# Remainder indices in a mixed-radix Fourier filter: one matrix per transform stage, in a kernel with a mixture of experts behind it

## The chip, the cores and the metric

The kernel runs on one core of a Trainium2 chip. The metric is the device time of one execution in microseconds (us). The core's engines, as the profile names them, are PE (TensorE: matrix products; PEld is its weight load), DVE (VectorE), ACT (ScalarE), POOL (GpSimd) and SP (SyncE, which here only issues DMAs, in the order of its queue). All data is 32-bit floating point.

## What is computed

The input `x` has 8 batches of 2496 tokens with 256 channels. First every channel of a batch is filtered along the tokens by a Fourier transform; then each token goes through the one expert, of eight, that its logits choose, and the result is weighted with the softmax value of that expert.

```python
X = np.fft.rfft(x, axis=1)                       # 8 x 2496 x 256
Y = X * (filt_r + 1j * filt_i)[None, :, :]
y = np.fft.irfft(Y, n=2496, axis=1).reshape(19968, 256)
logits = y @ w_gate                              # 256 x 8
e = np.argmax(logits, axis=1)
gate = softmax(logits)[token, e]                 # sum + 1e-9
out[token] = gate * (np.maximum(y[token] @ w1[e], 0) @ w2[e])   # 256 -> 1024 -> 256
```

## The kernel before

**Transform.** 2496 = 39 x 64 (`N1`, `N2`). Because `x` is real, 20 (`NF`) of the 39 frequencies of the short axis are enough. A batch passes four stages, each a set of matrix products with a constant matrix as the stationary operand:

- Stage A (`stage_a`, L344): the transform over 39, for three of the 64 offsets at a time, 22 columns (`NG`) of 117 rows in six chunks (`CH`); matrix `tas`, one for all columns; 512 moving elements per product. The result goes to DRAM (`zd`).
- Stage B (`stage_b`, L359): the transform over 64, for one frequency f of the 20 at a time. The twiddle factors are folded into the matrix, so `tbs` holds 20 matrices and each product moves 256 elements; two frequencies share a PSUM bank. DVE then multiplies by the filter `ht`: `ys` with the real part (L366), `yw` with the imaginary part in two halves of the partitions (L367, L368), and the sum of both at L370, on POOL in batch 0 and on DVE later.
- Stage C (`stage_c`, L382 and L384): back over 64, with `tcs`, which holds one matrix for f = 0 and one for the others, so the first pair is two products of 256 and the other nine pairs are one of 512. The result goes to DRAM (`ud`).
- Stage D (`stage_d`, L405): back over 39 with twiddles, 22 matrices in `tds`, products of 256 elements; the result lies in the buffers `yo` (tag "y", six of them).

Batch 0 doesn't go through DRAM: `first_a` (L424), `turn_z` (L441), `first_c` (L449) and `turn_u` (L464) turn the data with transposes on PE. Behind D come the logits (L491), the routing (`route`, small DVE instructions), and for each of a batch's columns a scatter of rows by POOL (L607) into `rowsd`, sorted by expert.

**Experts.** Tiles of 512, 256 or 128 sorted rows are read back (`xg`), transposed (L737), multiplied with `w1` (`hidden`, L744, with the ReLU on ACT at L748) and `w2` (`result`, L758), and the rows are scattered to `out` (L764).

**What sets the order.** PE, DVE, ACT and SP run an order that a planner writes while the program is built. It walks through `STEPS` (filter work: each has a place, a load that it needs, and a cost) and `experts()`; `now`, `credit` and `share()` decide which goes next. `more_loads` issues loads of `x`, `z` and `u` as long as fewer than `NIN` = 7 of them are held (buffers tag "in"); `halt` keeps steps that load `u` or use `y` back when all six `yo` buffers are held (`held_y[0] == 6`). POOL's order is set by the framework's scheduler. `load_filters(c)` runs between the steps of `first_a`: for four frequencies it loads part of `tbs` (L255), the real part of the filter (L256) and the imaginary part (L260, L262). `load_rest` loads `tds` (L267) and small constants.

Of the kernel before, what the change touches and what calls it, by code (L numbers as in the profile page):

```python
# [10 lines left out]
F32 = mybir.dt.float32  # L11
# [3 lines left out]
ALU = mybir.AluOpType  # L15
# [4 lines left out]
P = 128  # L20
S = 2496
D = 256
E = 8
F = 1024

N1 = 39
N2 = 64
NF = (N1 + 1) // 2
NS = 2 * NF

NB = 3
NG = 22
TP = NB * N1
TK = NB * NS
# [1 line left out]
FT = F // P  # L36


def dft_tables():

    w = 2.0 * np.pi
    q = np.arange(N1)
    t = np.arange(N2)
    g = np.arange(N2)  # L50
    half = N2 // 2
    sg = np.where(g < half, 1.0, -1.0)

    ta = np.zeros((NB, N1, NB, NS))
    for f in range(NF):
        ang = w * ((q * f) % N1) / N1
        for j in range(NB):
            ta[j, :, j, f] = np.cos(ang)
            if f:
                ta[j, :, j, NF + f] = -np.sin(ang)  # L60

    tb = np.zeros((2, N2, NF, 2, N2))
    for f in range(NF):
        ang = w * ((t[:, None] * (f + N1 * g)[None, :]) % S) / S
        c, sn = np.cos(ang), np.sin(ang)
        if f:
            tb[0, :, f, 0] = c
            tb[1, :, f, 0] = sn
            tb[0, :, f, 1] = -sn * sg
            tb[1, :, f, 1] = c * sg  # L70
        else:
            tb[0, :, f, 0, :half] = c[:, :half]
            tb[0, :, f, 1, 1:half] = -sn[:, 1:half]
            tb[0, :, f, 0, half] = (-1.0) ** t

    tc = np.zeros((2, N2, 2, 2, N2))
    ang = w * ((g[:, None] * t[None, :]) % N2) / N2
    c, sn = np.cos(ang), np.sin(ang)
    tc[0, :, 1, 0] = c
    tc[0, :, 1, 1] = sn  # L80
    tc[1, :, 1, 0] = -sn * sg[:, None]
    tc[1, :, 1, 1] = c * sg[:, None]
    tc[0, :half, 0, 0] = 2.0 * c[:half]
    tc[1, :half, 0, 0] = -2.0 * sn[:half]
    tc[1, 0, 0, 0] = 0.0
    tc[0, 0, 0, 0] = 1.0
    tc[0, half, 0, 0] = (-1.0) ** t

    td = np.zeros((NB, NS, NG, NB, N1))
    ids = np.zeros((NB, N1, NG))  # L90
    valid = np.zeros((NB, N1, NG))
    for j in range(NB):
        for i in range(len(range(j, N2, NB))):
            n = N2 * q + NB * i + j
            ids[j, :, i] = n
            valid[j, :, i] = 1.0
            td[j, 0, i, j] = 1.0 / S
            for f in range(1, NF):
                ang = w * ((n * f) % S) / S
                td[j, f, i, j] = 2.0 / S * np.cos(ang)  # L100
                td[j, NF + f, i, j] = -2.0 / S * np.sin(ang)

    return {
        "ta": ta.reshape(TP, TK),
        "tb": tb.reshape(P, NF, P),
        "tc": tc.reshape(P, 2, P),
        "td": td.reshape(TK, NG, TP),
        "ids": ids.reshape(TP, NG),
        "valid": valid.reshape(TP, NG),
    }  # L110


def lay_x(x):

    out = np.zeros((x.shape[0], P, NG, D), x.dtype)
    v = x.reshape(-1, N1, N2, D)
    for j in range(NB):
        n = len(range(j, N2, NB))
        out[:, j * N1:(j + 1) * N1, :n] = v[:, :, j::NB]
    return out  # L120


def lay_filter(fr, fi):

    g = np.arange(N2)[:, None]
    f = np.arange(NF)[None, :]
    k = f + N1 * g
    k = np.where(k <= S // 2, k, S - k)
    fr, fi = fr[k], fi[k]
    h = NF // 2  # L130
    return np.concatenate([np.concatenate([fr, fr]), np.concatenate([fi[:, :h], fi[:, h:]])], axis=1)
# [3 lines left out]
def kernel(  # L135
# [8 lines left out]
    tb: bass.AP,  # L144
    tcm: bass.AP,
    td: bass.AP,
    ids: bass.AP,
    valid: bass.AP,
    out: bass.AP,
):  # L150
    nc = tc.nc
    mm = nc.tensor.matmul
# [24 lines left out]
    DR = D + 16  # L177
# [15 lines left out]
    psr = fft.enter_context(tc.tile_pool(name="psr", bufs=1, space=PSUM))  # L193

    tas = cst.tile([TP, TK], F32, name="tas")
    tbs = cst.tile([P, NF, P], F32, name="tbs")
    tcs = cst.tile([P, 2, P], F32, name="tcs")
    tds = cst.tile([TK, NG, TP], F32, name="tds")

    ht = cst.tile([P, NF + NF // 2, D], F32, name="ht")  # L200

# [46 lines left out]
    HP = P // 2  # L248
# [3 lines left out]

    def load_filters(c):
        f0, n = FH[c]
        nc.sync.dma_start(out=tbs[:, f0:f0 + n], in_=tb[:, f0:f0 + n])  # L255
        nc.sync.dma_start(out=ht[:HP, f0:f0 + n], in_=filt[:HP, f0:f0 + n, :])  # L256
        half, f1 = divmod(f0, NF // 2)
        rows = slice(half * HP, (half + 1) * HP)
        nh = min(n, NF // 2 - f1)
        nc.sync.dma_start(out=ht[rows, NF + f1:NF + f1 + nh], in_=filt[rows, NF + f1:NF + f1 + nh, :])  # L260
        if nh < n:
            nc.sync.dma_start(out=ht[HP:, NF:NF + n - nh], in_=filt[HP:, NF:NF + n - nh, :])  # L262
        if c == 0:
            nc.sync.dma_start(out=tcs, in_=tcm)

# [33 lines left out]
            yield NS, slice(m, n), rows[(NG - 1) * TK:, :].rearrange("(i p) d -> p i d", p=NS)  # L299

    ins, outs, lgs, yts = {}, {}, {}, {}
    NIN = 7

    moves, stored = [[], []], set()

# [45 lines left out]
    def stage_b(b, f):  # L351
        c, j = divmod(f, 4)
        if b == 0:
            zi, j = outs.pop(("zi", f)), 0
        else:
            zi = ins["z", b, c] if j == 0 else ins.pop(("z", b, c))
        p = bank()
        for i in range(2):
            mm(p[:, i * D:(i + 1) * D], lhsT=tbs[:, f + i, :], rhs=zi[:, j + i, :], start=True, stop=True)  # L359

        z2 = p.rearrange("p (i d) -> p i d", i=2)
        ys = outs["y", b, f] = sb.tile([P, 2, D], F32, tag="ys", name="ys", bufs=3)
        yw = sb.tile([P, 2, D], F32, tag="yw", name="yw")
        half, f1 = divmod(f, NF // 2)
        fi = ht[half * HP:(half + 1) * HP, NF + f1:NF + f1 + 2, :]
        nc.vector.tensor_mul(ys, z2, ht[:, f:f + 2, :])  # L366
        nc.vector.scalar_tensor_tensor(out=yw[:HP], in0=z2[HP:], scalar=-1.0, in1=fi, op0=ALU.mult, op1=ALU.mult)  # L367
        nc.vector.tensor_mul(yw[HP:], z2[:HP], fi)  # L368

        (nc.gpsimd if b == 0 else nc.vector).tensor_tensor(ys, ys, yw, op=ALU.add)  # L370
        free["v"] = max(free["v"], now[0]) + (2.1 if b == 0 else 2.8)

    def stage_c(b, f):
        ys = outs.pop(("y", b, f))
        j = f % 4
        if j == 0:
            outs["u", b] = sb.tile([P, 4, D], F32, tag="st", name="uo", bufs=4)
        uo = outs["u", b]
        p = bank()
        if f == 0:  # L380
            for i in range(2):
                mm(p[:, i * D:(i + 1) * D], lhsT=tcs[:, i, :], rhs=ys[:, i, :], start=True, stop=True)  # L382
        else:
            mm(p, lhsT=tcs[:, 1, :], rhs=ys, start=True, stop=True)  # L384
        evac(uo[:, j:j + 2, :], p.rearrange("p (i d) -> p i d", i=2), 512)
        if j == 2:
            f0 = f - 2
            move(ud[b][:, f0:f0 + 4, :], uo[:HP])
            move(ud[b][:, NF + f0:NF + f0 + 4, :], uo[HP:])
        if f == NF - 2:  # L390
            mark(("c", b))

    def stage_d(b, c):
        if c == 0:
            lgs[b] = sb.tile([TP, NG, E], F32, tag="lg", name="lg")
        i0, n = CH[c]
        held_y[0] += 1
        ui = outs.pop(("ui", c)) if b == 0 else ins.pop(("u", b, c))
        yo = outs["o", b, c] = sb.tile([P, 4, DR], F32, tag="y", name="yo", bufs=6)[:TP]
        for j in range(0, n, 2):  # L400
            p = bank()
            for i in range(2):

                k = NS if i0 + j + i == NG - 1 else TK
                mm(p[:TP, i * D:(i + 1) * D], lhsT=tds[:k, i0 + j + i, :], rhs=ui[:k, j + i, :],  # L405
                   start=True, stop=True)
            evac(yo[:, j:j + 2, :D], p[:TP, :].rearrange("p (i d) -> p i d", i=2), 512)


# [34 lines left out]
    def first_c(f):  # L444
        ys = outs.pop(("y", 0, f))
        p = bank().rearrange("p (h i c t) -> p h i c t", h=DH, c=2, i=2)
        for i in range(2):
            for h in range(DH):
                mm(p[:, h, i].rearrange("p c t -> p (c t)"), lhsT=ys[:, i, h * P:(h + 1) * P],  # L449
                   rhs=tcs[:, min(f + i, 1), :], start=True, stop=True)  # L450
        for h in range(DH):
            evac(zu["u"][:, h, :, :, f:f + 2], p[:, h].rearrange("p i c t -> p t c i"), D)

# [55 lines left out]
    def route(b, g):  # L509
# [84 lines left out]
        if b == B - 1 and t0 + w == NG:  # L594
# [3 lines left out]
            nc.vector.tensor_tensor(padf, cnt, eoff, op=ALU.add)  # L598
            nc.vector.tensor_tensor(padf, padf, prow.to_broadcast((P, E)), op=ALU.add)
            nc.vector.tensor_copy(pad, padf)  # L600
            fill = sb.tile([P, 4, DR], F32, tag="y", name="fill", bufs=6)[:, 0]
            nc.vector.memset(fill, 0.0)
            nc.vector.memset(fill.bitcast(I32)[:, D:D + 8], N)
            rows += [(pad[:, e:e + 1], fill) for e in range(E)]
# [309 lines left out]
    with tc.manual_schedule(  # L914
# [8 lines left out]
        while f or e:  # L923
            asked = e and e[2] in when

            halt = f and f[2] and f[2][0] in "uy" and held_y[0] == 6
            if e and asked and (not f and not sides or when[e[2]] <= now[0] and (credit > 0.0 or not f or halt)):
                e[0]()
                now[0] += e[1]
# [51 lines left out]
```

## Time and profile before

| what | value |
|---|---|
| median of six runs | 1621.8 us (1617.55 to 1624.59) |
| the profiled execution | 1623.96 us |
| its span, first to last instruction | 1622.3 us |
| mean granted PE clock in it | 0.989 |
| PEld busy, ACT busy, DVE busy, POOL busy | 70%, 32%, 26%, 22% of the span |
| DMA: bytes, mean rate | 289.89 MB, 179 GB/s |
| DMA share from 0 to 40 us, rate | 0.97, 288 GB/s |

The engines' shares are of the whole span. A stretch of 40 us says more: PE is busy for 31.75 us of the first one, 33.64 of 80:120, 31.61 of 160:200 and 32.25 of 880:920, and for the whole 40 us of nearly every stretch after 320 us. The granted clock is 1.00 in most stretches, 0.90 in 80:120, 0.87 in 160:200 and 0.91 in 880:920. The DMA column is the mean share of the 16 DMA engines.

### The profile page before, as it was taken

What the parts mean: (1) busy time and instruction counts of PE and PEld (TensorE: products, weight loads), DVE (VectorE), ACT (ScalarE), POOL (GpSimd) and SP (SyncE); (2) the same over time, 40 slices, a digit from 0 to 9 for tenths busy, and PEclk for the clock granted to TensorE, in tenths of its full rate; (3) what the DMA queues carried; (4) which work ended last, traced back from release to release, by engine and by line L of the source; (5) the groups of instructions that cost most, each with busy time, mean ns of one, the idle gap of its engine ahead of it and who ended that gap; (6) DMA issues with size and microseconds to landing.
All of it is one profiled execution on the core that took longest, in us unless ns stands there. A gap on an engine that the chain in (4) does not pass through costs nothing.

```text
span 1622.3 us, 21714 instructions
## 1 busy us (share of the span) xinstructions
PE 1567.9 (97%) x7094; PEld 1139.8 (70%) x7094; DVE 422.9 (26%) x1418; ACT 519.0 (32%) x1149; POOL 357.2 (22%) x373
## 2 busy tenths in 40 slices
PE   7988889999999999999999899999999999999998
PEld 6645566787566666666666567667666678899997
DVE  4576561624512422135222212300000000000000
ACT  4434343433422232222233232222222222333433
POOL 1131322304213221024013205411111011111111
PEclk9989899999999999999999999999999999999999
DMA  9679696887945584357434624433444446565551
GB/s 286 184 212 286 211 320 214 248 263 233 296 128 163 164 255 135 115 155 189 141 110 128 183 79 150 151 109 112 137 148 154 132 147 226 184 216 183 173 181 46
DMA packets 119700, 289.89 MB, mean 179 GB/s; under 512 B 17387, under 2 KB 58484, under 8 KB 119469
## 3 DMA queue, kind: packets, MB, share of 16 engines
q1 hardware_dynamic: 100373, 245.18, 50.3%
q0 software_dynamic: 19216, 43.33, 7.7%
q8 instruction: 58, 0.95, 0.3%
q14 instruction: 53, 0.43, 0.1%
HBM read 208.44 MB, written 80.90 MB: 178 GB/s over the span
## 4 chain that ended last, share of the span: by engine, by line
PE 89%; DMA 4%; DVE 3%; issue 2%; SPq 1%; ACT 0%; POOL 0%; POOLq 0%; ACTq 0%; DVEq 0%
PE bank L758 34%; PE bank L744 34%; PE bank L405 4%; PE bank L359 3%; PE bank L344 3%; PE bank L384 3%; PE bank L737 2%; PE bank L477 2%; DMA fin<-zd 1%; PE lt L491 1%; DMA fin<-ud 1%; PE bank L424 1%; DVE yw L368 1%; DVE yw L367 1%; DVE ys L366 1%
## 5 line engine op out<-in xcount | busy, mean ns | idle before, releaser
L744 PE MATMUL bank<-xT,w1t 128*128 128x512 f32 (+2 forms) x2080 | 590.8, 436 | 1.1 <-issue 1.0
L758 PE MATMUL bank<-w2t,hT 128*128 128x256 f32 x2240 | 501.1, 380 | 1.3 <-issue 1.3
L744 PEld LDWEIGHTS bank<-xT,w1t 128*128 128x128 f32 x2080 | 338.3, 191 | 206.9 <-issue 184.6
L758 PEld LDWEIGHTS bank<-w2t,hT 128*128 128x128 f32 x2240 | 422.4, 191 | 67.7 <-issue 12.5
L764 POOL DMA_INDIRECT out_dram<-ys,idt x163 | 160.3, 984 | 917.6 <-ACT ys L763 625.4
L748 ACT ACTIVATE hT<-bank 128x512 f32<-128x512 f32 (+2 forms) x520 | 227.6, 439 | 366.7 <-PE bank L744 336.8
L607 POOL DMA_INDIRECT rows<-yo,row x176 | 174.7, 992 | 300.7 <-DVE row L587 68.4
L763 ACT ACTIVATE ys<-bank,gts 128x256 f32<-128x256 f32 x157 | 74.4, 474 | 495.4 <-PE bank L758 457.2
L241 DVE COPY xT<-bank 128x128 f32<-128x128 f32 (+2 forms) x53 | 25.1, 473 | 583.7 <-PE bank L737 469.2
L366 DVE TENSOR_TENSOR ys<-bank,ht 128x512 f32<-128x512 f32 x80 | 55.1, 689 | 130.8 <-PE bank L359 85.5
L405 PE MATMUL bank<-fin,tds 120*117 120x256 f32 (+1 forms) x308 | 76.7, 388 | 12.1 <-DMA fin<-ud 12.1
L758 PE MATMUL bank<-w2s,hT 128*128 x368 | 83.2, 379 | 0.0
L405 PEld LDWEIGHTS bank<-fin,tds 120*117 120x117 f32 (+1 forms) x308 | 55.4, 184 | 37.2 <-issue 19.8
L384 PE MATMUL bank<-ys,tcs 128*128 128x512 f32 x126 | 69.1, 631 | 9.4 <-DVE ys L370 5.7
L359 PE MATMUL bank<-fin,tbs 128*128 128x256 f32 x280 | 73.9, 387 | 0.9 <-DMA fin<-zd 0.7
L344 PE MATMUL bank<-fin,tas 117*120 117x512 f32 x154 | 74.1, 600 | 0.0
L758 PEld LDWEIGHTS bank<-w2s,hT 128*128 128x128 f32 x368 | 68.1, 190 | 8.3
L359 PEld LDWEIGHTS bank<-fin,tbs 128*128 128x128 f32 x280 | 52.5, 193 | 21.6 <-issue 15.6
L241 ACT COPY uo<-bank 128x512 f32<-128x512 f32 x70 | 41.1, 587 | 65.0 <-PE bank L384 43.3
L367 DVE SCALAR_TENSOR_TENSOR yw<-bank,ht 64x512 f32<-64x512 f32 x80 | 55.4, 693 | 1.1
L368 DVE TENSOR_TENSOR yw<-bank,ht 64x512 f32<-64x512 f32 x80 | 54.7, 684 | 1.1
L241 ACT COPY yo<-bank 117x512 f32<-117x512 f32 x70 | 40.7, 589 | 40.8 <-PE bank L405 37.6
(126 smaller groups left out, 874.0 us busy)
## 6 DMA issues: line engine op xcount, KB each, us to landing
w1t<-in_moe_w_dram SPq DMA_DIRECT2D x130, 512.0 KB
w2t<-in_moe_w_dram SPq DMA_DIRECT2D x84, 512.0 KB
fin<-in_x_dram SPq DMA_DIRECT2D x40, 512.0 KB
fin<-zd SPq DMA_DIRECT2D x70, 256.0 KB
ud<-uo SPq DMA_DIRECT2D x70, 256.0 KB
zd<-zo SPq DMA_DIRECT2D x35, 480.0 KB
fin<-ud SPq DMA_DIRECT2D x35, 480.0 KB
xg<-rows SPq DMA_DIRECT2D x28, 544.0 KB
```

The lines of the kernel that those rows point to most:

```text
L241: either(n, lambda: nc.vector.tensor_copy(o, i), lambda: nc.scalar.copy(out=o, in_=i))
L344: mm(p[:TK, :], lhsT=tas, rhs=xt[:TP, j:j + 2, :], start=True, stop=True)
L359: mm(p[:, i * D:(i + 1) * D], lhsT=tbs[:, f + i, :], rhs=zi[:, j + i, :], start=True, stop=True)
L367: nc.vector.scalar_tensor_tensor(out=yw[:HP], in0=z2[HP:], scalar=-1.0, in1=fi, op0=ALU.mult, op1=ALU.mult)
L384: mm(p, lhsT=tcs[:, 1, :], rhs=ys, start=True, stop=True)
L405: mm(p[:TP, i * D:(i + 1) * D], lhsT=tds[:k, i0 + j + i, :], rhs=ui[:k, j + i, :], start=True, stop=True)
L607: sc = nc.gpsimd.indirect_dma_start(out=rowsd, out_offset=bass.IndirectOffsetOnAxis(ap=at, axis=0), in_=what, in_offset=None,)
L744: mm(p[:, :m], lhsT=w1t[2 * i + k // FH2][:, dh, k % FH2 * P:(k % FH2 + 1) * P], rhs=xts[i][:, dh, :m], start=(dh == 0), stop=(dh == DH - 1))
L748: lambda: nc.scalar.activation(hT[:, :m], p[:, :m], AF.Relu))
L758: mm(p[:, :D], lhsT=hs[i][k][:, j * P:(j + 1) * P], rhs=w2, start=(k == 0), stop=(k == FT - 1))
L763: lambda: nc.scalar.activation(ys, p[:, :D], AF.Copy, scale=gate))
L764: nc.gpsimd.indirect_dma_start(out=out, out_offset=bass.IndirectOffsetOnAxis(ap=idt[i].bitcast(U32)[:, j, :], axis=0), in_=ys, in_offset=None,
```

## The change

The indices of tokens and of frequencies are taken by remainders (39 and 64 have no common factor), so that the transform over 2496 falls into one over 39 and one over 64 without twiddle factors between them. One matrix then serves all frequencies in stage B (`tbs`, 128 x 128), all in C (`tcs`), and all columns in D (`tds`, 120 x 117). `lay_x` and `ids`, on the host, put the tokens in the new order; the filter is laid out in the new order of the coefficients.

- B and D: two products of 256 elements become one of 512, except for the last pair of D's columns, whose two columns have different numbers of rows. C: f = 0 goes with the others.
- The conjugate half of the coefficients needs the other sign of the imaginary filter. A table `sg` of +1 and -1 is loaded, and POOL multiplies each loaded piece of the imaginary filter by it, in place.
- `NIN` goes from 7 to 8, the `yo` buffers from 6 to 8 (`YB`), and `halt` with them.

```diff
-    tbs = cst.tile([P, NF, P], F32, name="tbs")
-    tcs = cst.tile([P, 2, P], F32, name="tcs")
-    tds = cst.tile([TK, NG, TP], F32, name="tds")
+    tbs = cst.tile([P, P], F32, name="tbs")
+    tcs = cst.tile([P, P], F32, name="tcs")
+    tds = cst.tile([TK, TP], F32, name="tds")
+    sgs = cst.tile([P, NF // 2], F32, name="sgs")
...
     def load_filters(c):
         f0, n = FH[c]
-        nc.sync.dma_start(out=tbs[:, f0:f0 + n], in_=tb[:, f0:f0 + n])
+        if c == 0:
+            nc.sync.dma_start(out=tbs, in_=tb)
+            nc.sync.dma_start(out=sgs, in_=sg)
         nc.sync.dma_start(out=ht[:HP, f0:f0 + n], in_=filt[:HP, f0:f0 + n, :])
...
-        nc.sync.dma_start(out=ht[rows, NF + f1:NF + f1 + nh], in_=filt[rows, NF + f1:NF + f1 + nh, :])
+        parts = [(rows, slice(f1, f1 + nh), slice(NF + f1, NF + f1 + nh))]
         if nh < n:
-            nc.sync.dma_start(out=ht[HP:, NF:NF + n - nh], in_=filt[HP:, NF:NF + n - nh, :])
+            parts.append((slice(HP, P), slice(0, n - nh), slice(NF, NF + n - nh)))
+        for r, fs, at in parts:
+            nc.sync.dma_start(out=ht[r, at], in_=filt[r, at, :])
+            nc.gpsimd.tensor_tensor(
+                ht[r, at], ht[r, at], sgs[r, fs, None].to_broadcast((HP, fs.stop - fs.start, D)), op=ALU.mult
+            )
...
-    NIN = 7
+    NIN, YB = 8, 8
...
-        for i in range(2):
-            mm(p[:, i * D:(i + 1) * D], lhsT=tbs[:, f + i, :], rhs=zi[:, j + i, :], start=True, stop=True)
+        mm(p, lhsT=tbs, rhs=zi[:, j:j + 2, :], start=True, stop=True)
...
-        if f == 0:
-            for i in range(2):
-                mm(p[:, i * D:(i + 1) * D], lhsT=tcs[:, i, :], rhs=ys[:, i, :], start=True, stop=True)
-        else:
-            mm(p, lhsT=tcs[:, 1, :], rhs=ys, start=True, stop=True)
+        mm(p, lhsT=tcs, rhs=ys, start=True, stop=True)
...
-        yo = outs["o", b, c] = sb.tile([P, 4, DR], F32, tag="y", name="yo", bufs=6)[:TP]
+        yo = outs["o", b, c] = sb.tile([P, 4, DR], F32, tag="y", name="yo", bufs=YB)[:TP]
...
-            for i in range(2):
-
-                k = NS if i0 + j + i == NG - 1 else TK
-                mm(p[:TP, i * D:(i + 1) * D], lhsT=tds[:k, i0 + j + i, :], rhs=ui[:k, j + i, :],
-                   start=True, stop=True)
+            if i0 + j + 2 < NG:
+                mm(p[:TP, :], lhsT=tds, rhs=ui[:TK, j:j + 2, :], start=True, stop=True)
+            else:
+
+                for i, k in enumerate((TK, NS)):
+                    mm(p[:TP, i * D:(i + 1) * D], lhsT=tds[:k, :], rhs=ui[:k, j + i, :], start=True, stop=True)
...
-            halt = f and f[2] and f[2][0] in "uy" and held_y[0] == 6
+            halt = f and f[2] and f[2][0] in "uy" and held_y[0] == YB
```

The new tables on the host; `sgs` holds `sg`, by frequency, in two halves of the partitions:

```python
def token(q, t):
    return (q * N2 * pow(N2, -1, N1) + t * N1 * pow(N1, -1, N2)) % S
def coefficients():
    k = np.arange(S)
    of = np.zeros((N2, N1), int)
    of[k * pow(N1, -1, N2) % N2, k * pow(N2, -1, N1) % N1] = k
    return of[:, :NF]
...
    tb = np.block([[c, -sn], [sn, c]])
    tc = np.block([[c, sn], [-sn, c]])
...
    sg = np.where(coefficients() <= S // 2, 1.0, -1.0)
```

More of the change, by code (lines that the diff above doesn't have):

```diff
@@ L49, in dft_tables @@
     t = np.arange(N2)
-    g = np.arange(N2)
-    half = N2 // 2
-    sg = np.where(g < half, 1.0, -1.0)
     ta = np.zeros((NB, N1, NB, NS))
+    td = np.zeros((NB, NS, NB, N1))
     for f in range(NF):
@@ L58, in dft_tables @@
             ta[j, :, j, f] = np.cos(ang)
+            td[j, f, j] = (2.0 if f else 1.0) / S * np.cos(ang)
             if f:
                 ta[j, :, j, NF + f] = -np.sin(ang)
[L62 to L70, printed above, removed]
-        else:
[L72 to L77, printed above, removed]
-    c, sn = np.cos(ang), np.sin(ang)
[L79 to L89, printed above, removed]
+                td[j, NF + f, j] = -2.0 / S * np.sin(ang)
+    ang = w * ((t[:, None] * t[None, :]) % N2) / N2
+    c, sn = np.cos(ang), np.sin(ang)
+    tb = np.block([[c, -sn], [sn, c]])
+    tc = np.block([[c, sn], [-sn, c]])
     ids = np.zeros((NB, N1, NG))
@@ L93, in dft_tables @@
         for i in range(len(range(j, N2, NB))):
-            n = N2 * q + NB * i + j
-            ids[j, :, i] = n
+            ids[j, :, i] = token(q, NB * i + j)
             valid[j, :, i] = 1.0
[L97 to L101, printed above, removed]
+    sg = np.where(coefficients() <= S // 2, 1.0, -1.0)
     return {
         "ta": ta.reshape(TP, TK),
-        "tb": tb.reshape(P, NF, P),
-        "tc": tc.reshape(P, 2, P),
-        "td": td.reshape(TK, NG, TP),
+        "tb": tb,
+        "tc": tc,
+        "td": td.reshape(TK, TP),
+        "sg": np.concatenate([sg[:, :NF // 2], sg[:, NF // 2:]]),
         "ids": ids.reshape(TP, NG),
@@ L115, in lay_x @@
     out = np.zeros((x.shape[0], P, NG, D), x.dtype)
-    v = x.reshape(-1, N1, N2, D)
+    q = np.arange(N1)
     for j in range(NB):
-        n = len(range(j, N2, NB))
-        out[:, j * N1:(j + 1) * N1, :n] = v[:, :, j::NB]
+        for i in range(len(range(j, N2, NB))):
+            out[:, j * N1:(j + 1) * N1, i] = x[:, token(q, NB * i + j)]
     return out
 def lay_filter(fr, fi):
-    g = np.arange(N2)[:, None]
-    f = np.arange(NF)[None, :]
-    k = f + N1 * g
+    k = coefficients()
     k = np.where(k <= S // 2, k, S - k)
@@ L146 @@
     td: bass.AP,
+    sg: bass.AP,
     ids: bass.AP,
@@ L379, in stage_c @@
         p = bank()
-        if f == 0:
-            for i in range(2):
-                mm(p[:, i * D:(i + 1) * D], lhsT=tcs[:, i, :], rhs=ys[:, i, :], start=True, stop=True)
-        else:
-            mm(p, lhsT=tcs[:, 1, :], rhs=ys, start=True, stop=True)
+        mm(p, lhsT=tcs, rhs=ys, start=True, stop=True)
         evac(uo[:, j:j + 2, :], p.rearrange("p (i d) -> p i d", i=2), 512)
@@ L449, in first_c @@
                 mm(p[:, h, i].rearrange("p c t -> p (c t)"), lhsT=ys[:, i, h * P:(h + 1) * P],
-                   rhs=tcs[:, min(f + i, 1), :], start=True, stop=True)
+                   rhs=tcs, start=True, stop=True)
         for h in range(DH):
@@ L600, in route @@
             nc.vector.tensor_copy(pad, padf)
-            fill = sb.tile([P, 4, DR], F32, tag="y", name="fill", bufs=6)[:, 0]
+            fill = sb.tile([P, 4, DR], F32, tag="y", name="fill", bufs=YB)[:, 0]
             nc.vector.memset(fill, 0.0)
```

## Prediction

> **What bounds the kernel.** I read the page's first part, then the stretches of 40 us, then PE's waits, and last the timelines of the stages that the change touches.
>
> ```profile
> span 1622.3 us, 21714 instructions
> PE 1567.9 (97%) x7094; PEld 1139.8 (70%) x7094; DVE 422.9 (26%) x1418; ACT 519.0 (32%) x1149; POOL 357.2 (22%) x373
> ```
>
> PE is busy for 97% of the span: 1622.3 - 1567.9 = 54.4 us are idle. The mean clock of 0.989 costs another 0.011 x 1622 = 18 us. So nothing outside PE can be worth more than 72 us, and a change must either shorten PE's own stream or take idle time from it. Two thirds of the idle time lie before 320 us.
>
> **The merged products.** Batch by batch, 10 pairs in B (80 in all), 10 of 11 pairs in D (80) and the f = 0 pair of C in the seven later batches (7) become one product: 167 merges. A product shows as two matmul instructions (80 pairs of B were 320 of them), so 334 instructions go, and 334 weight loads. The page's means seem to say what this brings:
>
> ```profile
> L405 PE MATMUL bank<-fin,tds 120*117 120x256 f32 (+1 forms) x308 | 76.7, 388 | 12.1 <-DMA fin<-ud 12.1
> L384 PE MATMUL bank<-ys,tcs 128*128 128x512 f32 x126 | 69.1, 631 | 9.4 <-DVE ys L370 5.7
> L359 PE MATMUL bank<-fin,tbs 128*128 128x256 f32 x280 | 73.9, 387 | 0.9 <-DMA fin<-zd 0.7
> ```
>
> The last but one number is the mean of one instruction. Four of 387 ns are 1.55 us, two of 631 are 1.26, so a merge would save 0.29 us, and 167 of them 48 us. But 280 x 387 ns is 108 us where the line has 73.9 busy: the durations overlap, since each contains the time until its results are out. What counts is the distance from one start to the next, in PE's timeline of a dense stretch:
>
> ```profile
> 717.67 1.03 PE L359 MATMUL bank<-fin,tbs 128*128 128x256 f32 x4
> 718.53 1.88 PE L744 MATMUL bank<-xT,w1t 128*128 128x512 f32 x4
> 720.25 1.02 PE L384 MATMUL bank<-ys,tcs 128*128 128x512 f32 x2
> 721.11 2.31 PE L744 MATMUL bank<-xT,w1t 128*128 128x512 f32 x5
> ```
>
> Four of 256 (B, as it is) take 718.53 - 717.67 = 0.86 us, two of 512 (C, as B will be) 721.11 - 720.25 = 0.86. What is paid for is columns, and those stay. What an instruction costs beside its columns shows only in long runs of the chain:
>
> ```profile
> 689.63 3.44 PE bank L744 x8
> ...
> 701.21 3.46 PE bank L758 x16
> ```
>
> Eight of 512 and sixteen of 256 move the same columns in 3.44 and 3.46 us: 0.02 us for eight instructions, 2.5 ns each, with the rounding 1.2 to 3.8. 334 x 2.5 ns = **0.8 us less** (0.4 to 1.3). The removed weight loads lie beside products that last longer than they do (191 ns beside 215), so they give nothing more.
>
> **The order.** In the order of instructions of both kernels, DVE and ACT have the same rows in the same places, and PE differs by the merges alone. So the two more `yo` buffers never let a step go earlier: `halt` did not bind before. No copy into `yo` waits for a scatter of rows in the trace either. **YB: nothing.**
>
> **NIN 8.** On SP some loads move up by one place. A buffer gives PE something only where PE waits for a load:
>
> ```profile
> PE bank L405 <- DMA fin<-ud: 12.1, 5, 7.7
> ...
> PE bank L359 <- DMA fin<-zd: 0.7, 2, 0.5
> ```
>
> Of the 12.1 us, 7.75 lie at 904 us and 2.28 at 131 us. Both are a path through DRAM: SP waits until the last `ud` write has landed (at 899.16 and 126.32 us), then loads, and one buffer more starts neither. What is left, 1.8 + 0.7 = 2.5 us, is the most that an earlier load can give; zero is the least. I take **0.8 less**. It costs nothing where its cover fails: the eighth `x` load goes ahead of the filter's, and 4.58 MB instead of 4.25 are loaded up to the first imaginary piece. At 288 GB/s from SP's first `x` issue at 1.32 us that is an estimate of 17.2 us instead of 16.1, and DVE needs the piece at 21.59.
>
> **Less to load.** `tbs` 1280 KB, `tds` 1206.6 and `tcs` 128 become 64, 54.8 and 64, with 5 for `sg`: 2.4 MB less, 8.6 us of DMA time at the 288 GB/s of the first 40 us. PE waits for a load at 5.42 us (the first `x`, issued ahead of all this) and next at 130.98 us. The DMA time is hidden behind PE: **nothing**, and nothing to lose.
>
> **The sign on POOL.** This is the step that costs. POOL gets a product per filter piece: 64x1024 for c = 0, 1, 3, 4 and two of 64x512 for c = 2. It is not in the profile; the nearest row is POOL's add:
>
> ```profile
> 25.24 1.27 POOL L370 TENSOR_TENSOR ys<-ys,yw 128x512 f32<-128x512 f32 x1 [0.90 <-DVE yw L368]
> 28.69 1.28 POOL L370 TENSOR_TENSOR ys<-ys,yw 128x512 f32<-128x512 f32 x1 [2.18 <-DVE yw L368]
> ```
>
> By elements a piece costs the same 1.27 us, by elements per partition twice that, 2.54. I take T = 2.54, since DVE's rows go by the partition (64x512 at 693 ns, 128x512 at 689). DVE's rows with a broadcast operand (L525, 225 ns) cost the same as those without (L575, 225), so I add nothing for the broadcast.
>
> POOL's order in the changed kernel is: piece 0, adds of f = 0 and 2, piece 1, add of f = 4, piece 2 in two, add of f = 6, piece 3, add of f = 8, piece 4, then the rest. Piece 0 runs from 17.2 to 19.8 us, done before 21.59: hidden. Piece 1 (5.69 MB, so its data is there by about 21 us) stands behind the add that ends at 26.51, and DVE needs it at 27.22:
>
> ```profile
> 27.22 0.69 DVE L367 SCALAR_TENSOR_TENSOR yw<-bank,ht 64x512 f32<-64x512 f32 x1
> ```
>
> ```profile
> 30.71 1.06 PE L449 MATMUL bank<-tcs,ys 128*128 128x128 f32 x8
> ```
>
> L367 starts at 26.65 + T. From it to the end of the add took 2.75 us (27.22 to 29.97), so PE's L449 starts at 29.46 + T instead of 30.71: T - 1.25 later, **1.3 us** with 2.54 and 0 with 1.27. Queued behind L367 on DVE are L368, a copy of `ut` and L366 of f = 6; ACT's `ut` copy and `zi` follow them, 1.1 us late, still ahead of PE, which is 1.3 late by then. The next three L449 come 3.92, 3.92 and 4.01 us after one another; POOL needs T + 1.42 in each (piece, add, two gaps). With 2.54 that is 3.96: it fits, nothing is added. PE is full until 50 us and can't win the 1.3 back; the later idle times hang on chains that start later as well.
>
> A rule speaks against the step. DVE's 128x512 product takes 0.69 us where POOL's add takes 1.27. The Trainium skill (GPSIMD Engine Reference, "4.1 Engine selection") sends elementwise work with two inputs to VectorE, with GpSimd about twice as slow, and its section "3.1 Elementwise" has 4497 ns for 2048 elements per partition. Half of that, 2.25 us, would be its estimate of T, with a loss of 1.0 in place of 1.3.
>
> **Sum.** -0.8 - 0.8 + 0 + 0 + 1.3 = -0.3 us: 1623.7 for an execution like the profiled one (1623.96, of which 1622.3 is the span), and with the median 2.2 us lower, **1621.5 us**.
>
> **What idle time costs twice.** PE's clock falls after a gap: behind 1.77 us of idle at 753 us, sixteen matmuls of 256 took 4.79 us in the chain in place of 3.46; with the four matmuls before them (1.24 us from start to start in place of 0.87) 1.7 us are lost. I call this a clock dip. The Trainium skill (TensorE: Matmul & The Clock Gate, "Why this matters for your kernels") sets the limit at gaps above about 3 us; by it my 1.3 us would have no second cost. The row shows that less suffices, so I count 1.7 us per dip made or removed, and leave two of them, 3.4 us, on either side.
>
> **Rival, faster (0.25).** The shift of 1.3 us and the loads that come a step earlier change where idle time falls in 90 to 320 us. If the loads give their 2.5 us, merges 1.3, POOL nothing, and two clock dips go, it is -7.2: 1614.6. For it: these 230 us hold most of the dips. Against: the waits there are for DVE (ys L370, pos, oe), whose rows stay. In it is a small chance that the means are right after all (1574).
>
> **Rival, slower (0.20).** One mechanism: POOL's product stands in front of the add. From T = 2.5 on, each of the three later intervals adds T - 2.5 to the first T - 1.25. The loss passes 0.2% (3.2 us, with -1.6 from the rest) at T of 3.4 us; at 4 it is 2.75 + 4.5 - 1.6 = +5.6, 1627.4; at 5.1, if a stride of zero doubles the cost, 3.85 + 7.8 - 1.6 = +10, 1632. For it: no broadcast on POOL is in the trace. Against: DVE's rows.
>
> **That the change doesn't do what it says** holds for its buffers, as above; the forecast contains it.
>
> **Chances and range.** The forecast, with its clock dips on one side or the other, has 0.55 and stays within 0.2% (about what a measurement of this kernel tells from no change). Faster by more: 0.25; slower by more: 0.20. The range runs from the fast rival's end, 1614, to the slow rival with T of 4.3, 1629; what lies outside is POOL at 5 us and the means.
>
> **What would show it.** Right: B at 0.86 us per pair from start to start; PE's instruction count 334 lower and its busy time within 1.5 us; POOL's pieces at 2.3 to 2.6 us; L449 of f = 4 about 1.3 us behind its place. Wrong: pieces above 3.4 us, PE waiting for `fin` elsewhere than before, or a mean clock that differs from 0.989 by 0.003 or more, which moves the time by some 5 us.

## The result and the profile after

The changed kernel takes 1619.57 us (median of 32 runs, 1614.54 to 1625.05), the kernel before, run beside it, 1623.54 (74 runs, 1617.55 to 1631.02). The ratio is 0.998 [0.9973, 0.9988]: a gain of 0.2%, on the line that the prediction drew between "the same" and "faster". The forecast was 1621.5 with 1614 to 1629.

The profiled execution of the changed kernel, not among the 32, is the slowest on record, 1627.27 us, and that of before took 1623.96. Most of the difference goes with the mean granted clock: 0.985 against 0.989. In the 34 recorded runs of the changed kernel, the profiled one included, time falls by 1.3 us for each 0.001 of clock (correlation -0.89), so a difference of a few us between two profiled executions says nothing on the kernels. Below, stretches are compared with the loss to the slow clock taken out: half of PE's busy time in the stretches at half clock.

The head of the page, and the groups of stages D, C and B (line, engine, operation, form, count; busy us, mean ns of one; idle time before them and what ended most of it):

```profile
span 1625.6 us, 21005 instructions
...
PE 1572.3 (97%) x6760; PEld 1082.5 (67%) x6760; DVE 422.8 (26%) x1418; ACT 518.7 (32%) x1149; POOL 367.5 (23%) x379
...
L372 PE MATMUL bank<-ys,tcs 128*128 128x512 f32 x140 | 74.4, 613 | 13.5 <-DVE ys L362 10.2
...
L391 PE MATMUL bank<-fin,tds 120*117 120x512 f32 x140 | 70.6, 628 | 14.0 <-DMA fin<-ud 14.0
...
L351 PE MATMUL bank<-fin,tbs 128*128 128x512 f32 x140 | 72.4, 600 | 0.0
```

PE has 334 instructions and 334 weight loads fewer, and POOL six more. B's mean went from 387 to 600 ns while its busy time went from 73.9 to 72.4: the means compare nothing here. PE's busy time rose by 4.4 us, which the clock more than explains: products take nearly twice as long at half clock (eight of L405 in before 3.46 us at 904.52, 1.96 at 130.98), and half of the time that PE is busy at half clock is 23.0 us here against 15.9 before (the start, for which the profile has no clock, is counted as half). PE no longer waits for `zd` ahead of B (0.7 us before), but waits longer for DVE ahead of C: 10.2 us, where L384 and L382 had 8.6 together.

In PE's timeline (start, duration, line, form) a pair of B takes 0.87 us from its start to the next one's, and a pair of C 0.85, as before:

```profile
90.03 1.03 PE L351 MATMUL bank<-fin,tbs 128*128 128x512 f32 x2
90.90 1.02 PE L372 MATMUL bank<-ys,tcs 128*128 128x512 f32 x2
91.75 0.38 PE L491 MATMUL bank<-ident,ls 128*117 128x128 f32 x2
```

The new work on POOL, with the add of f = 4 between; the first DVE line is the product that needs piece 1, and the PE line is the stage C behind it:

```profile
17.71 1.89 POOL L253 TENSOR_TENSOR ht<-ht,sgs 64x1024 f32<-64x1024 f32 x1 [15.38 <-DMA ht<-in_filt_dram]
...
27.17 1.89 POOL L253 TENSOR_TENSOR ht<-ht,sgs 64x1024 f32<-64x1024 f32 x1
30.56 1.27 POOL L362 TENSOR_TENSOR ys<-ys,yw 128x512 f32<-128x512 f32 x1 [1.50 <-DMA tds<-in_td_dram]
31.79 2.15 POOL L253 TENSOR_TENSOR ht<-ht,sgs 64x512 f32<-64x512 f32 x2
...
29.09 0.69 DVE L359 SCALAR_TENSOR_TENSOR yw<-bank,ht 64x512 f32<-64x512 f32 x1 [1.26 <-POOL ht L253]
...
31.89 1.16 PE L438 MATMUL bank<-tcs,ys 128*128 128x128 f32 x8 [0.33 <-POOL ys L362]
```

This is the predicted chain, piece by piece: POOL's piece ends at 29.06, DVE's product starts at 29.09, POOL's add follows at 30.56, PE waits for it. Only its length differs: T is 1.89 us, not 2.54. (The add's releaser in the record, a DMA, can't be its own: its input comes from DVE, whose L360 ends at 30.48.) From start to start, PE's row ahead of this L438 is 0.68 us later than in before (30.96 against 30.28) and the row behind it 1.27 us later (32.88 against 31.61): 0.6 us are lost, which is T - 1.25.

### The profile page after: what moved, and what is told of

Its sections match the earlier page's. It is cut to its first block, busy times and chain, and to the rows that moved or that the text cites. A ratio compares the mean times of both kernels' runs of the same rounds, so it can differ in the third digit from the quotient of the medians.

```text
span 1625.6 us, 21005 instructions
## 1 busy us (share of the span) xinstructions
PE 1572.3 (97%) x6760; PEld 1082.5 (67%) x6760; DVE 422.8 (26%) x1418; ACT 518.7 (32%) x1149; POOL 367.5 (23%) x379
## 4 chain that ended last, share of the span: by engine, by line
PE 90%; DMA 3%; DVE 3%; issue 2%; SPq 0%; ACT 0%; POOL 0%; POOLq 0%; ACTq 0%; DVEq 0%
PE bank L747 34%; PE bank L733 34%; PE bank L391 4%; PE bank L351 3%; PE bank L337 3%; PE bank L372 3%; PE bank L726 2%; PE bank L466 2%; DMA fin<-ud 1%; PE lt L480 1%; DMA zd<-zo 1%; PE bank L413 1%; DMA ud<-uo 1%; DVE yw L360 1%; DVE yw L359 1%
## 5 line engine op out<-in xcount | busy, mean ns | idle before, releaser
L372 PE MATMUL bank<-ys,tcs 128*128 128x512 f32 x140 | 74.4, 613 | 13.5 <-DVE ys L362 10.2
L391 PE MATMUL bank<-fin,tds 120*117 120x512 f32 x140 | 70.6, 628 | 14.0 <-DMA fin<-ud 14.0
L351 PE MATMUL bank<-fin,tbs 128*128 128x512 f32 x140 | 72.4, 600 | 0.0
L391 PEld LDWEIGHTS bank<-fin,tds 120*117 120x117 f32 x140 | 25.9, 188 | 45.3 <-issue 35.5
L360 DVE TENSOR_TENSOR yw<-bank,ht 64x512 f32<-64x512 f32 x80 | 54.7, 683 | 1.1
L726 PEld LDWEIGHTS bank<-ident,xg 128*128 128x128 f32 x326 | 39.2, 143 | 20.5 <-issue 17.3
```

The costliest lines, as they stand in the source:

```text
L351: mm(p, lhsT=tbs, rhs=zi[:, j:j + 2, :], start=True, stop=True)
L372: mm(p, lhsT=tcs, rhs=ys, start=True, stop=True)
L391: mm(p[:TP, :], lhsT=tds, rhs=ui[:TK, j:j + 2, :], start=True, stop=True)
L726: nc.tensor.transpose(pt[:, j, :], xg[:, j, dh * P:(dh + 1) * P], ident)
```

## The experiments

Three theories were open. **Loads** ("L"): the eighth load buffer, with or without the two `yo` buffers, starts loads earlier and takes waits from PE. **Bytes**: 2.4 MB less to load leave DMA time to the rest. **What remains** when both are undone: merges ("M" in the expectations), minus the sign on POOL, and a shift of PE against the other engines. Each run is compared with the kernel before on the same chip. The runs went to three chips, here A, B and C; before takes 1610.8, 1623.0 and 1625.2 us on them.

**The kernel before, again** (chip A): what does the comparison make of no change?

> The kernel before, unchanged, run as if it were a changed one. It measures what a ratio of nothing looks like. Every theory: ratio 1.000, within 0.0010. Its profile shows which of PE's waits come again in the same place and length (a wait that differs by more than 0.3 us between two profiles of one kernel can't be used to compare two kernels) and how far the mean clock moves by itself: between 0.985 and 0.993.

1612.64 us, ratio 1.001 [0.9997, 1.0022]. So 0.1% is what no change can show. Its profile differs from the first one of the same kernel, which has

```profile
185.24 2.04 PE L384 MATMUL bank<-ys,tcs 128*128 128x512 f32 x2 [3.39 <-DVE ys L370]
...
240.70 0.42 PE L548 MATMUL rk<-oe,tri 117*117 117x64 f32 x2 [3.95 <-DVE oe L537]
```

where the one on chip A has

```profile
183.90 1.10 PE L384 MATMUL bank<-ys,tcs 128*128 128x512 f32 x2 [0.70 <-DVE mx L522]
...
232.38 0.42 PE L548 MATMUL rk<-oe,tri 117*117 117x64 f32 x2 [1.65 <-DVE oe L537]
```

The waits for `zd` at 141 and 153 us are gone too, without any change to the kernel. A wait of half a microsecond in one profile is not a property of the kernel.

**The buffers back** (chip A), all else as changed:

```diff
-    NIN, YB = 8, 8
+    NIN, YB = 7, 6
```

> The changed kernel with 7 load buffers and 6 y buffers, as before; the matrices, the merged products, the sign on POOL and the smaller loads stay. Theory L (the gain of 3 us is mostly the eighth load buffer: on SP the z loads come ahead of stores that wait for a copy, so PE's waits for loads and its gaps between 138 and 185 us go): ratio 0.9995 to 1.0005, and PE waits again for zd or ud near 141 to 160 us, 1 to 2 us in all. Theory M (merges 0.8 us, less bytes, and nothing from buffers): ratio stays at 0.998, no such waits.

1610.64 us, 0.9996 [0.9984, 1.0007]. The time is what theory L expected, but on this chip, as the next runs show, no version gains, so it decides nothing. The waits for `zd`, which L expected as well, did not come back; here before has none of them either.

**The buffers and the bytes back** (chip A): as the last, with loads as large as the old matrices into tiles that nothing reads:

```diff
...
+        nc.sync.dma_start(out=more[:, c, :], in_=filt[:, f0:f0 + 2, :].rearrange("p f d -> p (f d)"))
...
+        nc.sync.dma_start(out=last[:TK], in_=filt[:TK, :10, :])
```

> As the run with the old buffers, and the 2.4 MB of the large matrices are loaded as well, into tiles that nobody reads, at their old places on SP. Theory L: as the run with the old buffers, difference below 0.0005. A theory that the smaller loads bring the gain: 0.0010 to 0.0015 slower than that run. By the prediction's count no PE wait lies in the stretch of those loads, so I expect no difference.

1611.01 us, 1.0002 [0.9991, 1.0013], 0.4 us from the last: on chip A the bytes are hidden. On the chips where a gain was measured they were never put back.

**No sign** (chip A): POOL's product taken out.

```diff
-            nc.gpsimd.tensor_tensor(
-                ht[r, at], ht[r, at], sgs[r, fs, None].to_broadcast((HP, fs.stop - fs.start, D)), op=ALU.mult
-            )
```

> The changed kernel without the product with the sign table on POOL (the imaginary filter keeps the sign of the layout, so the filter of the conjugate half is left out of the computation). PE's wait of 0.33 us for the add of f = 4 goes and the stages of batch 0 end 0.5 to 0.7 us earlier: 0.9996 of the changed kernel, so about 0.9976 of the kernel before. If the product cost what the prediction had, 1.3 us, it would be 0.9972.

1612.32 us, 1.0005 [0.9991, 1.0019]. A miss: a gain was expected and none came. In its profile the wait at f = 4 is gone, as it should be, but 0.6 us is below what the comparison can tell. On chip A no version differs from before by more than noise; at equal clock (a fit of time on mean clock over the runs of the chip) the three are 0.2 to 0.8 us ahead of it, with a standard error of 0.5. The changed kernel itself was not run there.

**The changed kernel again** (chip B), to have it beside the next three:

> The changed kernel, unchanged, beside runs of the kernel before on one chip. If the gain of 0.2% belongs to the change: ratio 0.9970 to 0.9990, and at the same mean clock the changed kernel is 1 to 3 us ahead. If the run of the kernel before against itself (1.0010) shows the size of what chance and the clock do, the ratio may be anywhere from 0.9980 to 1.0005, and at the same mean clock it is 0.3 to 1.5 us ahead (merges 0.8, loads up to 2.5, sign on POOL -0.6).

1620.4 us, 0.9981 [0.9967, 0.9995]: the gain is there again.

**The sign three times** (chip B): POOL's product issued three times.

```diff
+            for _ in range(3):
                 nc.gpsimd.tensor_tensor(
                     ht[r, at], ht[r, at], sgs[r, fs, None].to_broadcast((HP, fs.stop - fs.start, D)), op=ALU.mult
                 )
```

> The changed kernel with the product with the sign table done three times (the result is the same). A piece of 64x1024 on POOL took 1.89 us in the profile, so POOL has 15 pieces and 6 adds up to the add of f = 10: 17.7 + 15 x 1.89 + 6 x 1.27 = 53.7 us in place of 43.1, so PE is 9 to 11 us late at that point, in batch 0. If PE can't win it back, as the prediction says: +9 to +11 us against the changed kernel, ratio to the kernel before about 1.005. If later idle time absorbs it: below +4 us.

1634.94 us, 1.0069 [1.0049, 1.0088], 14.5 us above the changed kernel; with the clock's part taken out (the same fit over the runs of chip B) 11.4, where 9 to 11 were expected. In the timeline the adds queue behind the pieces, and PE behind the adds (the row of 7.34 us is one product of 64x1024 and five of 64x512):

```profile
17.39 5.82 POOL L254 TENSOR_TENSOR ht<-ht,sgs 64x1024 f32<-64x1024 f32 x3 [15.06 <-DMA ht<-in_filt_dram]
...
30.98 7.34 POOL L254 TENSOR_TENSOR ht<-ht,sgs 64x1024 f32<-64x1024 f32 x6
38.39 1.26 POOL L363 TENSOR_TENSOR ys<-ys,yw 128x512 f32<-128x512 f32 x1
...
26.03 1.68 PE L439 MATMUL bank<-tcs,ys 128*128 128x128 f32 x8 [2.81 <-POOL ys L363]
39.71 2.08 PE L439 MATMUL bank<-tcs,ys 128*128 128x128 f32 x8 [5.54 <-POOL ys L363]
56.70 1.64 PE L439 MATMUL bank<-tcs,ys 128*128 128x128 f32 x8 [3.04 <-POOL ys L363]
```

The last stage C of batch 0 starts at 70.22 us instead of 54.24, 16 us late, and most of that stays to the end. So POOL's place is on the path that sets the end: this is the prediction's slower rival, made real with a longer T.

**Eleven load buffers** (chip B), which should have shown the loads' gain enlarged or nothing:

```diff
-    NIN, YB = 8, 8
+    NIN, YB = 11, 6
```

> The changed kernel with 11 load buffers, y buffers back at 6. If the eighth load buffer brought part of the gain by putting loads ahead of stores on SP, three more put them further ahead: PE's waits for zd, ud and xg between 125 and 170 us fall by another 1 us or more. By the prediction the waits left are paths through DRAM (stores, then loads), and nothing changes: within 0.0007 of the changed kernel.

1642.54 us, 1.012 [1.0096, 1.0144]: a miss, and the largest effect of all. First, the loads of `x` stand ahead of the filter's, so that piece 0 starts at 20.96 us instead of about 17.5, and PE waits for its add:

```profile
20.96 1.89 POOL L253 TENSOR_TENSOR ht<-ht,sgs 64x1024 f32<-64x1024 f32 x1 [18.62 <-DMA ht<-in_filt_dram]
...
25.67 1.98 PE L438 MATMUL bank<-tcs,ys 128*128 128x128 f32 x8 [2.69 <-POOL ys L362]
```

Second, SP issues in the order of its queue, and loads that are issued early stand ahead of stores. ACT's copies wait longer for the buffers that the stores hold, and PE waits for ACT; that it is the loads ahead of them that make the stores late is read from the program's order, not tested by itself. The waits (who, for whom: us in total, times, longest) of the eleven buffers, ACT's first, then PE's:

```profile
ACT uo L227 <- DMA zd<-zo: 38.5, 4, 12.0
...
PE bank L337 <- ACT uo L227: 12.4, 2, 6.4
...
PE bank L747 <- ACT uo L227: 3.2, 1, 3.2
```

and of the changed kernel on the same chip:

```profile
ACT uo L227 <- DMA zd<-zo: 8.2, 3, 3.6
```

Three more load buffers are a cost here, not a gain that is too small to see.

**The sign in pairs** (chip B): the product for two frequencies at a time, in the order in which they are needed, so that a piece delays an add by half as much.

```diff
-            nc.gpsimd.tensor_tensor(
-                ht[r, at], ht[r, at], sgs[r, fs, None].to_broadcast((HP, fs.stop - fs.start, D)), op=ALU.mult
-            )
         if c == 0:
+            sign(0)
+            sign(2)
             nc.sync.dma_start(out=tcs, in_=tcm)
...
+    def sign(f):
+        half, f1 = divmod(f, NF // 2)
+        r = slice(half * HP, (half + 1) * HP)
+        at = slice(NF + f1, NF + f1 + 2)
+        nc.gpsimd.tensor_tensor(ht[r, at], ht[r, at], sgs[r, f1:f1 + 2, None].to_broadcast((HP, 2, D)), op=ALU.mult)
...
+        if b == 0 and 2 <= f < NF - 2:
+            sign(f + 2)
```

> The changed kernel with the sign product for two frequencies at a time (64x512, about 1.07 us by the profile of the changed kernel, half of the 2.15 of the two pieces of c = 2), so that DVE at f = 4 waits for one half only. PE's wait of 0.33 us for the add of f = 4 goes. A gain of 0.3 to 0.7 us: not to be seen in the time, to be seen at that row. If the framework's order on POOL puts more pieces ahead of an add, the wait stays.

1618.32 us, 0.9974 [0.9958, 0.999]. The wait at f = 4 is gone: the add of f = 4 starts at 28.64, between two pieces.

```profile
26.11 2.03 POOL L262 TENSOR_TENSOR ht<-ht,sgs 64x512 f32<-64x512 f32 x2
28.64 1.27 POOL L367 TENSOR_TENSOR ys<-ys,yw 128x512 f32<-128x512 f32 x1 [0.50 <-DVE yw L365]
29.87 2.15 POOL L262 TENSOR_TENSOR ht<-ht,sgs 64x512 f32<-64x512 f32 x2
```

Its interval overlaps that of the changed kernel on that chip (0.9981): the profile shows the step, the time can't.

**Buffers one by one** (chip C). The changed kernel:

> The changed kernel once more, as the reference of the three runs beside it on the same chip. Ratio to the kernel before 0.997 to 0.9995: the two earlier comparisons gave 0.998 and 0.9981.

The load buffer back too, beside the `yo` buffers:

```diff
-    NIN, YB = 8, 8
+    NIN, YB = 7, 6
```

> The changed kernel with 7 load buffers and 6 y buffers, beside the changed kernel on one chip. Theory L (the eighth load buffer brings part of the gain, since z loads stand ahead of stores on SP): PE waits again for zd near 141 and 153 us, 0.5 to 1.5 us, and it is 1 to 3 us slower than the changed kernel. Rival (the eighth buffer gives nothing, since what PE wins at 141 to 155 us it loses to later stores, as the run with eleven buffers shows in the large): within 1 us of it; the gain is then the merges and what the clock makes of the shifted idle times.

The `yo` buffers alone back:

```diff
-    NIN, YB = 8, 8
+    NIN, YB = 8, 6
```

> The changed kernel with 6 y buffers and 8 load buffers. The order of the instructions is the same on every engine, and no copy into a y buffer waits for a scatter of rows in any profile: same as the changed kernel, within 1 us, and PE's waits at the same places.

The sign in pairs, with the edit shown above for it, and both kinds of buffers back:

```diff
-    NIN, YB = 8, 8
+    NIN, YB = 7, 6
```

> The changed kernel with the sign product in pairs of frequencies and 7 load and 6 y buffers: merges and smaller loads, the sign hidden, loads and stores on SP in the old order. If the eighth load buffer gives nothing: as fast as the run of the sign in pairs, 0.9970 to 0.9985 of the kernel before. If it does: 1 to 3 us slower than that.

In this order: 1621.37, 1620.08, 1621.17 and 1620.46 us; 0.9976 [0.9961, 0.9991], 0.9968 [0.9951, 0.9985], 0.9972 [0.9957, 0.9987] and 0.9964 [0.9949, 0.9979]. All four beat the kernel before, and none can be told from the others. Theory L falls: without the buffers the gain is as large, and with seven load buffers PE has no wait for `zd` here either, so that their absence in the changed kernel is not the eighth buffer's doing. The last version, which would leave the load buffer out and keep the sign off PE's path, beats before by 0.36%, and the changed kernel not by more than noise.

## Where the gain lies

The sum of what is known is -0.8 (merges) + 0.6 (sign) = -0.2 us. Measured were, for the changed kernel, 4.0 us in the first result, 2.6 on B and 3.8 on C, and for its versions on A nothing beyond noise. The difference was looked for stretch by stretch. One stands out: from PE's first transpose of `xg` (at 163.34 us in before) to the rank product that waits for `oe` (at 240.70). Its length, with PE's busy time at half clock counted at half, and PE's idle time in it:

| kernel | chip | length, us | idle, us |
|---|---|---|---|
| before (first profile) | first | 72.90 | 9.19 |
| changed (first profile) | first | 69.18 | 6.43 |
| changed | B, C | 69.71, 69.59 | 6.58, 6.68 |
| sign in pairs | B | 69.25 | 6.16 |
| NIN 7, YB 6; NIN 8, YB 6 | C | 70.56, 69.83 | 7.38, 6.57 |
| sign in pairs, NIN 7, YB 6 | C | 68.46 | 4.88 |
| sign three times; eleven load buffers | B | 69.93, 73.72 | 6.68, 10.13 |
| before | A | 66.05 | 3.17 |
| buffers back; bytes back; no sign | A | 66.01, 66.00, 66.00 | 3.21, 3.20, 3.21 |

On chip A the stretch is the same to 0.05 us in the four kernels, and no gain is to be seen. Elsewhere it is 2.3 to 4.4 us shorter than in the one profile of before in eight profiles of versions with the new matrices; with eleven load buffers, where PE also waits 3.2 us for ACT in it, it is longer. In size this fits the gain. Counted in the same way, the time ahead of the stretch is 156.8 us in before and 157.0, 158.3 and 155.6 in the three profiles of the changed kernel, and the time behind it 1376.7 against 1376.4, 1375.4 and 1376.2, so the rest of the execution shows no such difference.

What happens in it: POOL issues eight scatters of rows, and DVE's next filter product does not start meanwhile, though its input is there. In before's first profile PE's pair is done at 176.91, and DVE starts on it at 182.28, 1.8 us after POOL's eighth scatter:

```profile
175.88 1.03 PE L359 MATMUL bank<-fin,tbs 128*128 128x256 f32 x4
...
182.28 0.69 DVE L366 TENSOR_TENSOR ys<-bank,ht 128x512 f32<-128x512 f32 x1 [9.10 <-PE bank L744]
...
179.53 0.98 POOL L607 DMA_INDIRECT rows<-yo,row  x1 [0.30 <-issue]
```

The same kernel on chip A, with the scatters at the same time, has no such pause; DVE follows PE at once:

```profile
177.14 1.03 PE L359 MATMUL bank<-fin,tbs 128*128 128x256 f32 x4
...
178.20 0.69 DVE L366 TENSOR_TENSOR ys<-bank,ht 128x512 f32<-128x512 f32 x1 [3.77 <-PE bank L359]
...
179.47 0.99 POOL L607 DMA_INDIRECT rows<-yo,row  x1 [0.30 <-issue]
```

The pause is 5.4 us in before, 3.7 to 4.7 in seven of the profiles of changed versions off chip A, 0.5 in the eighth (the last of the experiments), 5.6 with eleven load buffers, and under 0.1 in the four of chip A. It is not the releaser that the record names: L744's product is not an input of L366.

**Shown** is the place, as far as one profile of before goes: the kernel before was profiled only once outside chip A, and how far its stretch varies there by itself is not known. **Argued only** is the reason: that the shift of PE by merges and sign puts its pair nearer to the end of the pause, so that less of it is waited out. It would cover a part alone: PE's idle time around the pause is 4.6 us in before and 3.2 to 4.0 in the seven, and the rest of the difference is mostly the wait for `oe` at the stretch's end, 3.95 us against 2.1 to 3.7. A rival that was not undone where the gain is are the smaller loads: they were put back on chip A only. Against them stands that in before the last of these matrices had been loaded by 57.7 us, when PE first used it, more than 100 us ahead of the stretch. Nor were the merges themselves undone. What holds DVE was not tried. The Trainium skill (SBUF — State Buffer, "SBUF: two separate sides") has an exclusive lock between DVE and GpSimd, for DVE operations in a two-port mode or with two inputs in SBUF; L366 has one of its two inputs in PSUM, and PE too has idle time there that nothing in the profile explains (0.98 us ahead of 180.72), so no run here shows that it is this.

## Why the prediction was right or wrong

- **Merges, -0.8: right.** 0.86 us per pair became 0.87 and 0.85. Matched product by product outside slow clock, the pairs before and the merged ones differ by some 2.3 ns per instruction that went, 0.77 us for 334.
- **YB, nothing: right.** NIN 8 with YB 6 gives 0.9972 where the changed kernel gives 0.9976.
- **NIN, -0.8: wrong.** The step that failed: "What is left, 1.8 + 0.7 = 2.5 us, is the most that an earlier load can give". (The rows give 2.1 and not 1.8 us beside the two waits that were set apart: 0.41, 0.50 and 1.16.) Those waits were taken for a property of the kernel, of which one buffer more would take a third; the same kernel's second profile has no `zd` wait, and taking the buffer back costs nothing: 0.9968 with seven beside 0.9976 with eight. The cover that the step named, the filter behind the `x` loads, is the one that failed with eleven buffers; the other cost, stores behind loads in SP's queue, was not seen.
- **Less to load, nothing: right** on chip A, within 0.4 us; on the other chips not tested.
- **The sign on POOL, +1.3: the mechanism right, T mis-sized.** T is 1.89 us (1.04 per 64x512), so 0.6 us. The estimate by the number of elements, 1.27, and that by elements per partition, 2.54, are both off by some 0.6 us; taking DVE's rule for POOL was the weak step. The Trainium skill (GPSIMD Engine Reference, "3.1 Elementwise"), by the estimate of 2.25 drawn from it, was nearer but still 19% too long. T three times as long cost 11.4 us, where the slower rival's formula, T - 1.25 and three times T - 2.5, gives 13.3 more.
- **The sum, -0.3.** With the corrected terms -0.2, so the time was met while more than 3 us outside the sum were missed: -0.3 was forecast, and the two medians run beside each other are 4.0 apart. That 1619.57 lies within 2 us of 1621.5 is in part luck, since the forecast was built on a median of 1621.8 for before, and beside the changed kernel before took 1623.54. As far as one profile of before shows, the missed part lies in 163 to 241 us, inside the region that the faster rival named, but it came neither by its loads nor by fewer slow stretches of the clock: half clock costs 23.0 us after and 15.9 before in the first profiles, and over the runs of chip B the mean clock is 0.988 in both. What makes it stays open.
- **The signs.** Right: PE's count, B from start to start. Wrong: PE's busy time within 1.5 us (it rose by 4.4 with the clock), pieces at 2.3 to 2.6 us, L449 1.3 us late. The profile's mean clock of 0.985 was named as a sign of being wrong, but single runs of this one kernel go from 0.985 to 0.993.

## What to carry to other kernels

A mean duration of pipelined products is no price: the distance from start to start is, and by it one product of 512 columns costs what two of 256 do, but for some 2 ns per instruction. Work moved to an idle engine was free here only where it stood behind the work that the path needs, in pieces small enough to fit between. Profile the kernel before twice, on more than one chip, before a wait of under a microsecond is counted as something to win.

## What the runs showed of the hardware

- In these profiles the granted clock is either full or half, and half in multiples of 3.41 us (3.41, 6.83, 10.24), but for the stretch behind the last product. In the changed kernel a slow stretch begins at 55.72 us, and in the 3.4 us before it PE had rested for 0.47 and 1.13 us, no longer. The Trainium skill (TensorE: Matmul & The Clock Gate, "HAM oscillation — how this bites in real kernels") puts the rule at gaps above some 3.4 us; here only shorter ones went ahead of a slow stretch, though not always: before's first profile has rests of 0.52 and 1.08 us in that place and no slow stretch there.
- The kernel before differs by 12 to 14 us between chip A and the two others, more than three times what the change is worth, at mean clocks of 0.991 (A) and 0.988 (C). By 1.2 us for 0.001, the fit over the runs of C, the clock explains about 4 of the 14 us between these two.
- POOL's product with a broadcast operand takes 1.89 us for 64x1024 and 1.04 for 64x512, its add 1.27 for 128x512: neither the elements nor the elements per partition alone set the time. As the operation and the broadcast differ too, what does is not shown.
